# The last tile pair of an fp32-exact MLP: a PSUM bank of its own for one quarter of the result, and bias and residual rows added one chunk pair earlier

## The chip, the cores and the metric

One core of a Trainium2 chip runs the whole program. The metric is device time in microseconds (us), the median of several executions; a single profiled execution supplies the rows that are read here. In the rows, PE is the matrix engine, PEld its weight loads, DVE the vector engine, ACT the scalar engine, POOL the engine that issues one DMA queue, SP the engine that issues another.

## The reference

A transformer block on 2048 tokens of width 640: layer norm with a modulation from `c`, linear attention of 32 heads, a gated residual, then a second layer norm and the MLP. Only the MLP's end is touched:

```
h = jnp.einsum("bsd,df->bsf", x, w1) + b1        # F = 1728
r = jnp.where(h > 0, h, 0);  h = r * r
out = jnp.einsum("bsf,fd->bsd", h, w2) + b2
x = x + gb * out                                  # gb: one row of 640, from c and w_mod
```

## The kernel before

**Tiling.** The MLP works on pairs `j` of token tiles, 8 pairs (`NB`) of 2 x 128 tokens. For each pair the 1728 hidden features are taken in 14 chunks `f` of 128 (the last of 64), two at a time: chunk pair `n` is chunks `2n` and `2n+1`, seven chunk pairs (`NP`) for each `j`. `up(j, f)` makes one chunk of hidden features on PE (15 matmuls of 256 columns; 10 for the last chunk), adds the bias and applies relu on ACT (L1250), squares on DVE (L1251). `split_a` splits the result into a high part (ACT, L1274 and following) and a low part (DVE, L88) because every fp32 product is made of three matmuls, high x high, high x low and low x high (`three`). The tiles that hold these parts are called `ra`, and `ft` before the split. The second product, with `w2`, runs one chunk pair behind and adds into PSUM accumulators.

**Accumulators.** The output of a pair is cut into four quarters, named by letters: `"2"` (tile 0, the 384 left columns), `"3"` (tile 0, the 256 right columns), `"4"` (tile 1, left), `"x"` (tile 1, right). Most chunk pairs use a scheme with seven products instead of eight (`down_pair`), with three further accumulators `"1"`, `"5"`, and `"6"`/`"7"`, whose sums `first_combos` later adds onto the quarters in SBUF, rows `y_0` and `y_1`. For the last pair, `j` = 7, the last three chunk pairs (`n` = 4, 5, 6; `LAST` = 3) use the plain eight products (`down_plain`, and `last_downs` for `n` = 5 and 6). `acc(j, reg)` gives the accumulator of a name. Names of 384 columns have a bank (512 fp32 columns) each; `"3"` and `"x"` share one bank, tile `acc3x` (pool tag `p3x`), and `"6"` and `"7"` share one (tag `p67`). The framework places a wait between an engine that writes a tile and another that reads it; `"3"` and `"x"` are one tile.

**The end of the program.** The engine order is written by hand (`manual_schedule`), in the order of the calls in the loop over `j` and `n`. For `j` = 7 the steps that matter are these, in the words of the kernel:

- `residual(j)` at `n` = 3 puts two DMAs into SP's queue (L1405) that load the residual rows `xr_7_0` and `xr_7_1` (128 x 640 each).
- `add_bias(j, i)` at `n` = 5 adds the prepared row `bb` (gate times b2) to each on DVE.
- `first_combos(j)` at the end of `n` = 4 makes `y_0`, `y_1` from `"1"`, `"5"`, `"6"`, `"7"` (ACT L1424, L1425, then four DVE adds).
- at `n` = 5, `by_gate` (L1418) multiplies both `y` rows by the gate row `gb_b`.
- at `n` = 6, after both `up` and the splits, `add(Y, Y, XR)` (L1415) adds the residual rows to both `y` rows.
- `last_downs` then runs PE through `n` = 5 for `"3"`, `"x"`, `"2"`; `n` = 6 for `"3"`, `"x"`, `"2"`; and `n` = 5 and 6 for `"4"`. As each quarter is complete, DVE multiplies it by the gate into tile `end` (L1418, reading PSUM) and adds it to `y` (L1415), and SP stores it (L1412):

```
        for r in regs:
            if r[0] == "4":
                part(NP - 2, *r)
                at = 0
            part(NP - 1, *r)
            m = r[2].stop - r[2].start
            out_(*r, u[:, at : at + m])
            at += m
```

One line number can belong to many calls: L1415 is every `add`, L1418 every `by_gate`, L78 every matmul, L88 every low part.

Of the kernel before, what the change touches and what calls it, by code (L numbers as in the profile page):

```python
# [8 lines left out]
F32 = mybir.dt.float32  # L9
# [6 lines left out]
P = 128  # L16
# [21 lines left out]
PLAIN = 2  # L38
# [13 lines left out]
def kernel(  # L52
# [23 lines left out]
    def mm(o, terms, first=True, last=True, skip=False):  # L76
        for i, (a, b) in enumerate(terms):
            nc.tensor.matmul(  # L78
                o, a, b,
                start=first and i == 0, stop=last and i == len(terms) - 1,  # L80
                skip_group_check=skip,
            )

    def three(ah, al, bh, bl):
        return [(ah, bh), (ah, bl), (al, bh)]
# [52 lines left out]
    def tp(name):  # L138
        return psA.tile([P, 512], F32, tag="tp", name=name)
# [574 lines left out]
    for t in range(2, NT - 2):  # L714
        j, i = divmod(t, 2)
# [379 lines left out]
    NB = NT // 2  # L1095
# [126 lines left out]
    psC = ctx.enter_context(tc.tile_pool(name="psC", bufs=1, space=PS, reuse_waits="tile"))  # L1222
# [9 lines left out]
    def up(j, f):  # L1232

        n, k = FS[f], f % 2
        alone = j < PLAIN or (j, f) == (NB - 1, NF - 1)
        p = UP2[:, :256] if k and j < PLAIN else tp("up13")[:, :256] if k and alone else UP[:, 256 * k : 256 * k + 256]
        terms = []
        for d in range(NC):
            if n == P:
                terms += three(W1[f][:, 0, d], W1[f][:, 1, d], H2[j][:, d, 0], H2[j][:, d, 1])  # L1240
            else:
                terms += [(W1[f][:, 0, d], H2[j][:, d, 0]), (W1[f][:, 0, d], H2[j][:, d, 1])]
        mm(p, terms, first=(k == 0 or alone), skip=True)
        if k == 0:
            FT[j, f // 2] = p3.tile([P, 8, P], F32, tag="ft", name=f"ft{j}_{f // 2}", bufs=2)
        t = FT[j, f // 2]
        r = t[:, A12 : A22 + 1] if k else t[:, 0:8:7]
        p = p.rearrange("p (i n) -> p i n", i=2)
        if n == P:
            nc.scalar.activation(r, p, AF.Relu, bias=b1_t[:, f : f + 1])  # L1250
            nc.vector.tensor_tensor(r, r, r, op=ALU.mult)  # L1251
        else:
            u = t[:n, S1 : S2 + 1]
            nc.scalar.activation(u, p[n:], AF.Identity, bias=b1_t[n:, f : f + 1])
            nc.vector.tensor_tensor(u, p[:n], u, op=ALU.add)
            nc.vector.scalar_tensor_tensor(r[:n], u, 0.0, u, op0=ALU.max, op1=ALU.mult)

    def plain(j, n):
        return j < PLAIN or n == NF // 2 - 1 or j == NB - 1 and n >= NF // 2 - LAST
# [27 lines left out]
    def split_s(j, n):  # L1287
        t = FT[j, n]
        a = RS[j, n] = p3.tile([P, 2, 4, P], F32, tag="rs", name=f"rs{j}_{n}").bitcast(F32R)
        nc.scalar.activation(a[:, 0], t[:, S1 : S4 + 1], AF.Copy)  # L1290
        lo(a[:, 1], t[:, S1 : S4 + 1], a[:, 0])
# [18 lines left out]
    def t_load(n):  # L1310
        TR_[n] = [row("s1", f"traw{n}_{r}") for r in range(2)]
        for r in range(2):
            f = 2 * n + r
            nc.sync.dma_start(TR_[n][r], w2[f * P : (f + 1) * P])
# [48 lines left out]
    ACC, XR, Y, FIRST = {}, {}, {}, set()  # L1363

    def acc(j, reg):

        bank_ = {"3": "3x", "x": "3x", "6": "67", "7": "67"}.get(reg, reg)
        if (j, bank_) not in ACC:
            if len(bank_) == 2:
                ACC[j, bank_] = psC.tile([P, 512], F32, tag=f"p{bank_}", name=f"acc{bank_}_{j}")  # L1370
            else:
                ACC[j, bank_] = psA.tile([P, 512], F32, tag="pj", name=f"acc{bank_}_{j}", bufs=4)
        t = ACC[j, bank_]
        return (j, bank_), t[:, :384] if len(bank_) == 1 else t[:, 256:] if reg in "x7" else t[:, :256]
# [32 lines left out]
    def add_bias(j, i):  # L1407
        add(XR[j, i], XR[j, i], bb)
# [5 lines left out]
    def add(o, a, b):  # L1414
        nc.vector.tensor_tensor(o, a, b, op=ALU.add)  # L1415

    def by_gate(o, a, c):
        nc.vector.tensor_tensor(o, a, gb_b[:, c], op=ALU.mult)  # L1418
# [56 lines left out]
    def prep(n):  # L1475
        p_hi(n)
        p_lo(n)
        p_load(n)
# [52 lines left out]
    for j in range(NB):  # L1531
        if j <= PLAIN:
            if j:
                by_hand.__exit__(None, None, None)
            by_hand = tc.manual_schedule(engines={ET_.PE, ET_.DVE, ET_.Activation, ET_.Pool} | ({ET_.SP} if j != 1 else set()))
            by_hand.__enter__()
        for n in range(NP):
            down = lambda k: prev and (down_plain if plain(*prev) else down_pair)(*prev, k)
            twice = not plain(j, n)
            m = NP * j + n - NP - 1  # L1540
            if (j, n) == (NB - 1, NP - 1):
                for k in range(2):
                    up(j, 2 * n + k)
                    split_a(j, n, (k,))
                for i in range(2):
                    add(Y[j][i], Y[j][i], XR[j, i])
                break
            done = j - 1 if j and prev else None
            up(j, 2 * n)
            if prev and not plain(*prev):  # L1550
                split_s(*prev)
            down(0)
            if j < PLAIN:
                layer(j + 1, 2 * n, None if j else 0)
            if 0 < m < NP - 2:
                t_split(m - 1)
            if m == -1:
                t_load(0)
            if (j, n) == (PLAIN, 0):
                t_fetch(4)  # L1560
            if j >= PLAIN:
                if n == 5 + (j == PLAIN):
                    for i in range(2):
                        add_bias(j, i)
                layer(j + 1, 2 * n)
            prep(next(PREPS, 0))
            if j == 0:
                layer(j + 1, 2 * n, 1)
            if n == 0 and j:
                if j - 1 >= PLAIN:  # L1570
                    first_combos(j - 1)
                else:
                    Y[j - 1] = [row("s2", f"y{j - 1}_{i}") for i in range(2)]
                for r, i, c in (("3", 0, R), ("2", 0, L)):
                    end(j - 1, r, i, c)
            if n == 1 and j:
                gate(j - 1, 0)
                if j != PLAIN:
                    finish(j - 1, j < PLAIN)
            if n == 1 and j == PLAIN:  # L1580
                finish(j - 1, 0)
            if n == 2 and j == PLAIN:
                t_sums(NP - 2)
            if n == (2 if j > PLAIN else 1) and j:
                gate(j - 1, 1)
            if n == (5, 5, 5, 3)[min(j, 3)]:
                residual(j)
            for i in range(2):
                if n == 6 and j == 0:
                    add_bias(j, i)  # L1590
            if j == NB - 1 and n == 1:
                for k in range(NP - LAST, NP - 1):
                    plain_load(k)
            if j == NB - 1 and n == 3:
                for k in range(NP - LAST, NP - 1):
                    plain_split(k)
            if j == NB - 1 and n == NP - 2:
                for i in range(2):
                    by_gate(Y[j][i], Y[j][i], slice(0, D))
            up(j, 2 * n + 1)  # L1600
            if j >= PLAIN and n == 0:
                down(1)
            split_a(j, n)
            if twice:
                sums(j, n)
            if j < PLAIN or n:
                down(1)
            if m == NP + 1:
                t_split(NP - 2)
            ahead = (j, n) == (0, 3)  # L1610
            if ahead:
                layer(j + 1, 2 * n + 1)
            prep(next(PREPS, 0))
            if n == 0 and j:
                end(j - 1, "4", 1, L)
                end(j - 1, "x", 1, R)
            if n == (2 if j > PLAIN else 1 if j == PLAIN else 0) and j:
                finish(j - 1, j >= PLAIN)
            if not ahead:
                layer(j + 1, 2 * n + 1)  # L1620
            if 0 <= m < NP - 2:
                t_sums(m)
            if m == NP - 2:
                t_split(m - 1)
            if 0 < m + 1 < NP - 1:
                t_load(m + 1)
            if m == NP - 1:
                for i in range(2):
                    add_bias(j - 1, i)
            if j == NB - 1 and n == NP - LAST:  # L1630
                first_combos(j)
            prev = j, n
# [60 lines left out]
```

## Time and profile before

| what | before |
|---|---|
| median of 3 runs (lowest to highest) | 769.94 us (769.52 to 769.98) |
| the profiled execution, its own time | 769.86 us |
| its span in the profile | 768.2 us |
| PE busy | 759.3 us, 99% of the span |
| DVE busy | 593.8 us, 77% |
| ACT busy | 434.6 us, 57% |
| share of the chain that ended last: PE, DVE | 85%, 8% |

The profiled execution's span is 1.7 us shorter than its time; what lies around the span is taken to be the same for both kernels. A timeline row gives start and length of a merged group in us, engine, line, operation, what it writes and reads, its shape and count, and in brackets the idle time of the engine before it and what ended that. PE rows overlap because matmuls are pipelined: the length of a group is from the first start to the last end.

### The profile page before, as it was taken

The page shows a single profiled execution, that of the slowest core. Times are in us where ns is not written, and L with a number is a line of the kernel's source. Part 1 is how long each engine was busy: PE and PEld are TensorE (multiplying, and loading weights), DVE is VectorE, ACT ScalarE, POOL GpSimd, SP SyncE. Part 2 cuts the span into 40 slices and gives each one's busy share as a digit, 9 for nine tenths or more (in the row PEclk, how much of TensorE's full clock was granted, in tenths as well). Part 3 has the DMA queues.
Part 4 walks back from the last instruction along what each step waited for, and adds up shares of the span by engine and source line. Part 5 has one row for each costly group of instructions (what it writes and reads, how often), then busy time and mean ns, then how long its engine had stood idle before and what let it go on. Part 6 is the DMA issues. An engine that isn't in the chain of part 4 may idle for free.

```text
span 768.2 us, 15300 instructions
## 1 busy us (share of the span) xinstructions
PE 759.3 (99%) x5967; PEld 739.8 (96%) x5967; DVE 593.8 (77%) x1083; ACT 434.6 (57%) x971; POOL 144.2 (19%) x301
## 2 busy tenths in 40 slices
PE   9999999999999999999999999999999999999997
PEld 8999999999999989888999999999999999999996
DVE  6598897989999999999565667866767666675666
ACT  5766756767843454545776647465553636445331
POOL 3001101101100255442101000231321313222110
PEclk9999999999999999999999999999999999999999
DMA  9811431343333344155356367996766758766450
GB/s 327 305 65 73 137 103 54 104 139 114 119 104 109 117 142 170 70 80 160 107 180 222 110 226 253 286 323 195 226 181 197 232 177 262 221 184 192 130 165 35
DMA packets 52151, 126.69 MB, mean 165 GB/s; under 512 B 7335, under 2 KB 8103, under 8 KB 52079
## 3 DMA queue, kind: packets, MB, share of 16 engines
q1 hardware_dynamic: 34744, 84.65, 33.1%
q0 software_dynamic: 14752, 35.76, 16.7%
q10 hardware_dynamic: 2583, 5.30, 1.8%
q8 instruction: 47, 0.77, 0.4%
q14 instruction: 25, 0.20, 0.1%
HBM read 95.70 MB, written 29.89 MB: 163 GB/s over the span
## 4 chain that ended last, share of the span: by engine, by line
PE 85%; DVE 8%; issue 2%; DMA 2%; POOL 2%; ACT 1%; SPq 0%; POOLq 0%; DVEq 0%
PE up L78 23%; PE acc L78 17%; PE pk L78 9%; PE pv L78 9%; PE pq L78 8%; PE pwo L78 5%; PE acc3x L78 5%; PE kvp L450 3%; DVE dn L879 2%; DVE scr L877 2%; DVE ezb L901 1%; PE tb L357 1%; PE te L921 1%; DMA ring_b<-td_b 1%; PE ta L357 1%
## 5 line engine op out<-in xcount | busy, mean ns | idle before, releaser
L78 PE MATMUL up<-h,w 128*128 128x256 f32 x1640 | 206.4, 278 | 0.0
L78 PEld LDWEIGHTS up<-h,w 128*128 128x128 f32 x1640 | 196.1, 188 | 0.0
L1250 ACT ACTIVATE ft<-up,b_t 128x256 f32<-128x256 f32 x104 | 48.9, 470 | 115.1 <-PE up L78 114.6
L78 PE MATMUL acc<-w,ra 128*128 128x384 f32 x452 | 97.4, 335 | 0.0
L1251 DVE TENSOR_TENSOR ft<-ft 128x256 f32<-128x256 f32 x104 | 44.1, 424 | 51.2 <-ACT ft L1250 49.6
L78 PE MATMUL pwo<-wo,ot 128*128 128x256 f32 (+3 forms) x512 | 80.8, 312 | 0.6 <-DVE ot L88 0.6
L78 PEld LDWEIGHTS pwo<-wo,ot 128*128 128x128 f32 (+1 forms) x512 | 74.5, 188 | 3.8 <-issue 2.7
L78 PE MATMUL pq<-wq,hT 128*128 128x384 f32 (+1 forms) x480 | 75.2, 312 | 0.0
L78 PEld LDWEIGHTS acc<-w,ra 128*128 128x128 f32 x452 | 72.7, 188 | 0.7 <-DVE ra L88 0.5
L78 PE MATMUL pk<-wk,hT 128*128 128x384 f32 (+1 forms) x480 | 72.7, 308 | 0.0
L78 PE MATMUL pv<-wv,hT 128*128 128x384 f32 (+1 forms) x480 | 71.7, 307 | 0.0
L78 PEld LDWEIGHTS pq<-wq,hT 128*128 128x128 f32 x480 | 71.1, 188 | 0.6 <-issue 0.2
L78 PEld LDWEIGHTS pk<-wk,hT 128*128 128x128 f32 x480 | 70.5, 188 | 0.4 <-issue 0.2
L78 PEld LDWEIGHTS pv<-wv,hT 128*128 128x128 f32 x480 | 70.1, 188 | 0.0
L88 DVE TENSOR_TENSOR ra<-ft,ra 128x384 fp32r<-128x384 f32 (+2 forms) x86 | 36.8, 448 | 32.9 <-ACT ra L1274 20.2
L78 PE MATMUL acc3x<-w,ra 128*128 128x256 f32 x248 | 42.3, 278 | 1.4 <-DVE end L1418 1.4
L1360 POOL DMA_DIRECT2D ring_a<-td_a x34 | 18.3, 537 | 125.5 <-PE acc L78 103.2
L1274 ACT ACTIVATE ra<-ft 128x384 fp32r<-128x384 f32 x48 | 25.2, 526 | 28.4 <-DVE ft L1251 22.4
L78 PEld LDWEIGHTS acc3x<-w,ra 128*128 128x128 f32 x248 | 39.5, 188 | 1.8 <-DVE end L1418 1.6
L1265 DVE TENSOR_TENSOR ft<-ft 128x128 f32<-128x128 f32 x136 | 33.3, 286 | 1.2
L441 DVE TENSOR_REDUCE sk<-ek 128x64 f32<-128x1280 f32 x16 | 23.7, 1484 | 12.4 <-ACT ek L436 10.8
L885 POOL TENSOR_TENSOR dn<-dn,rs_q 128x32 f32<-128x32 f32 x32 | 20.1, 629 | 68.1 <-DVE dn L879 67.8
(264 smaller groups left out, 1406.5 us busy)
## 6 DMA issues: line engine op xcount, KB each, us to landing
ring_c<-td_c POOLq DMA_DIRECT2D x34, 384.0 KB, 4.0
ring_a<-td_a POOLq DMA_DIRECT2D x34, 384.0 KB, 4.1
ring_b<-td_b POOLq DMA_DIRECT2D x34, 256.0 KB, 4.0
esp<-eq SPq DMA_DIRECT2D x12, 640.0 KB, 3.2
el<-esp SPq DMA_DIRECT2D x12, 640.0 KB, 4.0
rw<-in_w SPq DMA_DIRECT2D x23, 320.0 KB, 3.1
wm<-in_w_mod SPq DMA_DIRECT2D x20, 320.0 KB, 3.7
xb<-in_x SPq DMA_DIRECT2D x8, 640.0 KB, 4.0
```

What stands on the lines that cost most here:

```text
L78: nc.tensor.matmul(o, a, b, start=first and i == 0, stop=last and i == len(terms) - 1, skip_group_check=skip,)
L88: (eng or nc.vector).tensor_tensor(out_lo, full, hi.bitcast(F32), op=ALU.subtract)
L357: nc.tensor.transpose(p[:, i * P : (i + 1) * P], xn[:, i, d * P : (d + 1) * P], ident)
L441: nc.vector.tensor_reduce(s, heads(flat(e)), axis=AX.X, op=ALU.add)
L450: nc.tensor.matmul(kvp[g // 4][64 * c : 64 * c + 64, a : a + 2 * n].rearrange("p (s n) -> p s n", s=2), v[:, u], e[:, :, o : o + n], start ...
L877: nc.vector.tensor_tensor(z, flat(ET[t]), flat(zb), op=ALU.mult)
L885: nc.gpsimd.tensor_tensor(dn[:, s], dn[:, s], rs[:, 1 - s], op=ALU.mult)
L1250: nc.scalar.activation(r, p, AF.Relu, bias=b1_t[:, f : f + 1])
L1251: nc.vector.tensor_tensor(r, r, r, op=ALU.mult)
L1265: nc.vector.tensor_tensor(t[:, o], t[:, a], t[:, b], op=op)
L1274: nc.scalar.activation(a[:, 0, :3], t[:, :3], AF.Copy)
L1360: nc.gpsimd.dma_start(RING[j, n, r], TD[n][r].bitcast(F32R))
```

## The change

`acc` gives quarter `"x"` of the last pair a tile of its own, `accx`, in the bank of the tag `p67`, which `"6"` and `"7"` of that pair have left after `first_combos`. `add_bias` of the last pair goes from `n` = 5 to `n` = 4 (there it stands behind the low part of `split_s` and ahead of `up(7, 9)`'s square). The addition of the residual rows goes from `n` = 6 to `n` = 5, each right behind its `by_gate`. No instruction is added or removed; pairs 0 to 6 are untouched.

```diff
     def acc(j, reg):
 
+        if (j, reg) == (NB - 1, "x"):
+            if (j, reg) not in ACC:
+                ACC[j, reg] = psC.tile([P, 512], F32, tag="p67", name="accx")
+            return (j, reg), ACC[j, reg][:, :256]
         bank_ = {"3": "3x", "x": "3x", "6": "67", "7": "67"}.get(reg, reg)
@@
                     up(j, 2 * n + k)
                     split_a(j, n, (k,))
-                for i in range(2):
-                    add(Y[j][i], Y[j][i], XR[j, i])
                 break
@@
             if j >= PLAIN:
-                if n == 5 + (j == PLAIN):
+                if n == 5 + (j == PLAIN) - (j == NB - 1):
                     for i in range(2):
                         add_bias(j, i)
@@
             if j == NB - 1 and n == NP - 2:
                 for i in range(2):
                     by_gate(Y[j][i], Y[j][i], slice(0, D))
+                    add(Y[j][i], Y[j][i], XR[j, i])
```

On PE the place is the end of the program, from the first products of `ra_6` (`n` = 6) on: `"3"`, then `"x"`. Before, with the semaphores that each row waits for:

```order
L78 MATMUL acc3x_9076<-w_12_5160,ra_6_9396 128x256 [waits Activation_49]
L78 MATMUL acc3x_9076<-w_12_5160,ra_6_9396 128x256
L78 MATMUL acc3x_9076<-w_12_5160,ra_6_9396 128x256 [waits DVE_49]
L78 MATMUL acc3x_9076<-w_13_5163,ra_6_9396 128x256 [waits DVE_49]
L78 MATMUL acc3x_9076<-w_13_5163,ra_6_9396 128x256
L78 MATMUL acc3x_9076<-w_12_5160,ra_6_9396 128x256 [waits DVE_49]
L78 MATMUL acc3x_9076<-w_12_5160,ra_6_9396 128x256 x2
L78 MATMUL acc3x_9076<-w_13_5163,ra_6_9396 128x256 x2
```

The sixth row is the first product of `"x"` in this chunk pair; it waits on DVE for the read of `"3"` out of the same tile. The same place in the changed kernel:

```order
L78 MATMUL acc3x_9076<-w_12_5160,ra_6_9399 128x256 [waits Activation_49]
L78 MATMUL acc3x_9076<-w_12_5160,ra_6_9399 128x256
L78 MATMUL acc3x_9076<-w_12_5160,ra_6_9399 128x256 [waits DVE_49]
L78 MATMUL acc3x_9076<-w_13_5163,ra_6_9399 128x256 [waits DVE_49]
L78 MATMUL acc3x_9076<-w_13_5163,ra_6_9399 128x256
L78 MATMUL accx<-w_12_5160,ra_6_9399 128x256 x3
L78 MATMUL accx<-w_13_5163,ra_6_9399 128x256 x2
```

The order of the products is the same; those of `"x"` write `accx` and carry no wait. The first product of `"x"` altogether stands in chunk pair 5 (it is the second product of `n` = 4), where it now waits on DVE for `first_combos`.

On DVE the first place is chunk pair 4, around the squares of `up(7, 8)` and `up(7, 9)` (both `ft_4`) with the low part of `split_s` (`rs_3`) between them. Before:

```order
L1251 TENSOR_TENSOR ft_4_9253<-ft_4_9253 128x2x128
L88 TENSOR_TENSOR rs_3_9256<-ft_3_9175,rs_3_9256 128x512
L1251 TENSOR_TENSOR ft_4_9253<-ft_4_9253 128x256
L88 TENSOR_TENSOR ra_4_9285<-ft_4_9253,ra_4_9285 128x384
L88 TENSOR_TENSOR ra_4_9285<-ft_4_9253,ra_4_9285 128x128
```

In the changed kernel:

```order
L1251 TENSOR_TENSOR ft_4_9253<-ft_4_9253 128x2x128
L88 TENSOR_TENSOR rs_3_9256<-ft_3_9175,rs_3_9256 128x512
L1419 TENSOR_TENSOR xr_7_0_9192<-xr_7_0_9192,bb 128x640
L1419 TENSOR_TENSOR xr_7_1_9194<-xr_7_1_9194,bb 128x640
L1251 TENSOR_TENSOR ft_4_9253<-ft_4_9253 128x256
L88 TENSOR_TENSOR ra_4_9287<-ft_4_9253,ra_4_9287 128x384
L88 TENSOR_TENSOR ra_4_9287<-ft_4_9253,ra_4_9287 128x128
```

The two bias additions, each behind its own DMA, now stand ahead of the second square (`add` is L1419 there). The second place on DVE is chunk pair 5, between its two squares (`ft_5`). Before:

```order
L1251 TENSOR_TENSOR ft_5_9325<-ft_5_9325 128x2x128
L1415 TENSOR_TENSOR xr_7_0_9192<-xr_7_0_9192,bb 128x640
L1415 TENSOR_TENSOR xr_7_1_9194<-xr_7_1_9194,bb 128x640
L1418 TENSOR_TENSOR y_0_9302<-y_0_9302,gb_b 128x640
L1418 TENSOR_TENSOR y_1_9303<-y_1_9303,gb_b 128x640
L1251 TENSOR_TENSOR ft_5_9325<-ft_5_9325 128x256
```

In the changed kernel:

```order
L1251 TENSOR_TENSOR ft_5_9327<-ft_5_9327 128x2x128
L1422 TENSOR_TENSOR y_0_9304<-y_0_9304,gb_b 128x640
L1419 TENSOR_TENSOR y_0_9304<-y_0_9304,xr_7_0_9192 128x640
L1422 TENSOR_TENSOR y_1_9305<-y_1_9305,gb_b 128x640
L1419 TENSOR_TENSOR y_1_9305<-y_1_9305,xr_7_1_9194 128x640
L1251 TENSOR_TENSOR ft_5_9327<-ft_5_9327 128x256
```

Two rows have left and two have come from the end, so four rows of 640 columns stand here as before, the additions each behind the gate product whose result they read. At the end, the read of `"3"` into `end` follows the last low part (`ra_6`) directly; the two additions that stood between them are gone. ACT, POOL and SP have the same rows in the same order.

## The prediction

> **What bounds the kernel now.** I read the page's busy shares first, then the waits of the last 28 us, then the chain that ended last, then single rows of the end. The shares:
>
> ```profile
> PE 759.3 (99%) x5967; PEld 739.8 (96%) x5967; DVE 593.8 (77%) x1083; ACT 434.6 (57%) x971; POOL 144.2 (19%) x301
> ```
>
> PE has no spare time to speak of, so an edit gains only where PE stands, or behind PE's last matmul. The waits in the window from 740 us on give, of all engines, for PE only this (engine and line, waited for: total, times, longest):
>
> ```profile
> PE acc3x L78 <- DVE end L1418: 1.4, 1, 1.4
> ```
>
> One stop, of PE behind DVE's gate product. The chain that ended last shows what that stop consists of (start, length):
>
> ```profile
> 758.03 0.42 DVE ra L88
> 758.45 0.03 issue
> 758.48 1.56 DVE y L1415 x2
> 760.04 0.34 DVE end L1418
> 760.38 0.04 issue
> 760.43 0.84 PE acc3x L78 x5
> 761.26 2.79 PE acc L78 x16
> 764.05 0.02 issue
> 764.07 0.57 DVE end L1418
> ```
>
> The reader is to see that the chain leaves PE for two DVE steps, the two residual additions (758.48) and the read of "3" (760.04), and comes back to the five products of "x". The timeline rows of the same place:
>
> ```profile
> 758.00 1.00 PE L78 MATMUL acc3x<-w,ra 128*128 128x256 f32 x5
> 758.50 0.30 PEld L78 LDWEIGHTS acc3x<-w,ra 128*128 128x128 f32 x2 [0.20 <-DVE ra L88]
> 759.96 0.42 DVE L1418 TENSOR_TENSOR end<-acc3x,gb_b 128x256 f32<-128x256 f32 x1
> 760.41 0.42 DVE L1415 TENSOR_TENSOR y<-y,end 128x256 f32<-128x256 f32 x1
> 760.43 0.84 PE L78 MATMUL acc3x<-w,ra 128*128 128x256 f32 x5 [1.43 <-DVE end L1418]
> 761.30 0.43 DVE L1418 TENSOR_TENSOR end<-acc3x,gb_b 128x256 f32<-128x256 f32 x1 [0.47 <-PE acc3x L78]
> 761.76 0.42 DVE L1415 TENSOR_TENSOR y<-y,end 128x256 f32<-128x256 f32 x1
> 762.16 0.56 DVE L1418 TENSOR_TENSOR end<-acc,gb_b 128x384 f32<-128x384 f32 x1
> 762.76 0.56 DVE L1415 TENSOR_TENSOR y<-y,end 128x384 f32<-128x384 f32 x1
> ```
>
> PE ends "3" at 759.00, stands 1.43 us, and runs "x" from 760.43 to 761.27.
>
> **The change, part by part. The bank.** "x" no longer waits for the read of "3". The idle 1.43 us goes. That isn't all: a group that starts from a standstill is slower than one that follows others. A flowing group and the first matmul after the stop:
>
> ```profile
> 755.60 1.52 PE L78 MATMUL acc3x<-w,ra 128*128 128x256 f32 x12
> 760.43 0.38 PE L78 MATMUL acc3x<-w,ra 128*128 128x256 f32 x1 [1.43 <-DVE end L1418]
> L78 PE MATMUL acc3x<-w,ra 128*128 128x256 f32 x248 | 42.3, 278 | 1.4 <-DVE end L1418 1.4
> ```
>
> The twelve take 1.52 us, and one matmul of this shape lasts 278 ns on average (the third row, of the page's costliest groups), so the ends are (1.52 - 0.28) / 11 = 0.113 us apart. In flow the five of "x" would end 5 x 0.113 = 0.57 us behind those of "3", at 759.57; now they end at 761.27. The gain on PE is **1.70 us**: 1.43 of idle time and 0.27 of restart (0.84 - 0.57, the first matmul alone 0.38). The bounds: 1.43, if the restart is only a matter of how ends are modelled and comes back elsewhere, and 1.70. I take 1.70, since the chain's own row for "x" has 0.84, and the last low part (758.45) is already in when the five would start.
>
> On the restart a rule of the Trainium skill gives another figure. "TensorE: Matmul & The Clock Gate", in its sections on single matmul latency and on the back-to-back issue gap, puts a lone warm matmul of N columns at (398 + N) / 2.4 ns and the following ones N / 2.4 + 2.5 ns apart: an estimate of 272 and 109 ns for N = 256. By it the restart costs 0.16 us and the sum would be 1.59 us. The spacing agrees with the trace's 113 ns; the first matmul after the stop does not, 0.38 us here, and the trace decides.
>
> The other 16 products follow in 2.79 us as now: 759.57 + 2.79 = 762.36 instead of 764.05. Nothing new holds them: the operands of "2" and "4" were made before.
>
> **The wait that is added.** The first product into accx waits for first_combos, since the bank was that of "6" and "7". Rows of chunk pair 5:
>
> ```profile
> 746.79 1.83 DVE L1415 TENSOR_TENSOR y<-y,acc 128x256 f32<-128x256 f32 x4
> 747.63 0.68 PE L78 MATMUL acc<-w,ra 128*128 128x384 f32 x3
> 751.56 0.51 PE L78 MATMUL acc3x<-w,ra 128*128 128x256 f32 x3
> ```
>
> first_combos ends at 748.62, the first product of "x" runs at 751.56: 2.9 us of cover. If it were gone, everything on PE would queue behind it.
>
> **The bias rows, one chunk pair earlier.** Two DVE additions of 640 columns, whose place in chunk pair 4 is a hole:
>
> ```profile
> 742.41 0.69 DVE L88 TENSOR_TENSOR rs<-ft,rs 128x512 fp32r<-128x512 f32 x1
> 745.09 0.43 DVE L1251 TENSOR_TENSOR ft<-ft 128x256 f32<-128x256 f32 x1 [1.99 <-ACT ft L1250]
> 746.11 0.76 DVE L88 TENSOR_TENSOR ra<-ft,ra 128x384 fp32r<-128x384 f32 x2 [0.59 <-PE acc L78]
> 748.88 1.55 DVE L1415 TENSOR_TENSOR xr<-xr,bb 128x640 f32<-128x640 f32 x2
> 750.35 1.55 DVE L1418 TENSOR_TENSOR y<-y,gb_b 128x640 f32<-128x640 f32 x2
> 751.82 0.42 DVE L1251 TENSOR_TENSOR ft<-ft 128x256 f32<-128x256 f32 x1
> ```
>
> They take 1.55 us and DVE stands idle for 1.99 us from 743.10. They cost nothing if the residual rows have landed by 745.09 - 1.55 = 743.54. Behind that lies more cover: the low parts of pair 4 end at 746.87 and PE's first product with them starts at 747.63, 0.76 us later, so the limit is a landing at 744.30. SP's issues, the landing times of such transfers on the page, and the DMA traffic:
>
> ```profile
> 735.79 1.10 SPq L1405 DMA_DIRECT2D xr<-x  x2
> xr<-x SPq DMA_DIRECT2D x16, 320.0 KB, 4.6
> rawv<-in_wv SPq DMA_DIRECT2D x5, 320.0 KB, 10.6
> 742.00:743.00 1.00, 1.00 (x8) 1.00 (x8) 0.91 (x2) 0.38 (x1) 0.00 (x0) 1.00 0.20 47
> 743.00:744.00 1.00, 1.00 (x11) 1.00 (x10) 0.11 (x1) 0.00 (x0) 0.00 (x0) 1.00 0.02 6
> 744.00:745.00 1.00, 1.00 (x9) 1.00 (x9) 0.00 (x0) 0.41 (x1) 0.00 (x0) 1.00 0.00 0
> ```
>
> The second issue starts at about 736.34; with the median of 4.6 us it lands at 740.9. The last number of a window row is GB/s: from 744.00 on nothing is moving, so no landing is later than that. Cost 0 at both bounds, because even 744.00 is ahead of 744.30.
>
> **The residual additions, from the end into chunk pair 5.** There the bias rows have left, so four rows of 640 columns stand there as before, from 748.88 to the square at 751.82. Two of them now follow the row that they read. Rows that depend on each other start 0.04 us after the end (762.16 + 0.56, then 762.76), independent ones start 0.73 us apart (1.55 - 0.82). So 2 x 0.86 + 2 x 0.73 = 3.18 us against 2.94: the square comes 0.24 us later and ends at 752.48. Who waits for it is ACT:
>
> ```profile
> 752.97 0.53 ACT L1274 ACTIVATE ra<-ft 128x384 fp32r<-128x384 f32 x1 [1.25 <-PE acc3x L78]
> ```
>
> ACT waits for PE to leave the old ra until 752.97, so 0.49 us of cover hide it. At the end, 1.56 us of DVE in front of the read of "3" go: it starts at 759.03 instead of 759.96. With the distances of the rows above (0.45, 0.40, 0.46, 0.40, 0.60, and 0.56 for the last) DVE's six steps for "3", "x", "2" start at 759.03, 759.48, 759.88, 760.34, 760.74 and 761.34 and end at 761.90. "4" is complete at 762.36: DVE is ready 0.46 us ahead, PE sets the end, and all of the 1.70 arrives. The last addition ends at 763.52 instead of 765.22; the last store behind it stays as it is.
>
> **Sum** against the profiled execution: 769.86 - 1.70 = 768.16 us. That execution is 0.08 us under the median of the runs shown; against the median it is 768.24. I forecast **768.2**, 0.22% less.
>
> **Rivals.** *The restart is no gain:* only the idle time of 1.43 goes, 769.86 - 1.43 = 768.4. For it: ends of matmuls are modelled; against: DVE's read of "x" starts at 761.30, an event of another engine that confirms the end at 761.27. Chance 0.14.
>
> *The wait stays in another form* (the change does not do what it says: "x" still starts behind the read of "3"). Then only the additions help: the read ends at 759.45, "x" starts at 759.50 instead of 760.43, gain 0.93, 768.9. Against: the rows of the changed order carry no such wait. Chance 0.06. Its mirror image, where the additions still stand in front of the read of "3" in time, would let PE finish "4" at 762.36 but DVE come to "4" only at 759.96 + 0.45 + 0.40 + 0.46 + 0.40 + 0.60 + 0.60 = 762.87 instead of 764.07: gain 1.20, 768.7. Chance 0.04.
>
> *Slower: the residual rows are late.* DVE works in order, so an addition that waits for its DMA holds the square, the split and then PE. Each us of landing behind 744.30 is a us of PE. The gain is used up at 746.00. If they took what the slowest weight loads took, 10.6 us, they would land at 746.9: 2.6 us of stall, 0.9 net, 770.8. Against: the windows above show the transfers over by 744.00. Chance 0.04.
>
> **How the numbers follow.** My forecast has the other 0.72. A measurement of this kernel can tell about 0.2% from no change, 1.54 us, which is a time under 768.4, and the forecast lies only 0.16 us beyond. Within my own case I give four chances in five of landing under it, since the three runs shown lie within 0.46 us (0.58); the first rival lies just on the other side of the line (0.02 of its 0.14), the next two are inside it, and the slow rival is mostly inside it as well (0.11% at its price; half of its chance goes beyond). Faster by over 0.2%: 0.60; within: 0.38; slower: 0.02. The range is from 767.9, the forecast with the scatter of runs, to 768.9, which takes in both bounds of the restart and the rival in which the wait stays.
>
> **What would show each step.** The changed profile should have no PE wait on DVE end; the group of "x" should merge with that of "3" on PE without idle time; the residual additions should stand in front of the square of chunk pair 5, ending by 752.5, and the bias additions in the hole before 745.1, with no DMA wait named; the read of "3" should start within 0.1 us of 759.0, and DVE should wait for PE before the last gate product by about 0.5 us; the last addition should end about 1.70 us ahead of its old place. Wrong would be: an idle time of DVE in front of the bias rows, a PE wait around 747.6 or 751.6, a DVE row for "4" that starts later than 762.4, or a last store that takes longer to land.

## The result, and the profile after

| | before | after |
|---|---|---|
| median of 11 runs each (lowest to highest) | 769.98 us (769.07 to 771.25) | 767.88 us (767.04 to 768.97) |
| the profiled execution, its span | 769.86 us, 768.2 us | 767.73 us, 766.0 us |

The ratio is 0.9976, 95% interval 0.9968 to 0.9984: the change makes the kernel faster by 0.24%, 2.1 us between the medians (the interval is 1.2 to 2.5 us). The forecast was 768.2 us. Two executions of those below, one of "x" last and one of the kernel before, took twice as long (1537 and 1538 us; in the one with a trace, 25 matmuls of `up` take 6.05 us against 3.00) and enter no comparison.

The waits of the last 26 us of the changed kernel no longer contain a wait of the matmuls for DVE; instead the gate products on DVE (L1422 in this kernel, the additions are L1419) wait for PE, twice 0.6 us:

```profile
DVE end L1422 <- PE acc L78: 0.6, 1, 0.6
DVE end L1422 <- PE acc3x L78: 0.6, 1, 0.6
```

The chain that ended last now stays on PE until "4" is complete:

```profile
757.71 0.34 PE acc3x L78 x3
758.06 0.00 issue
758.06 0.51 PE acc3x L78 x2
758.57 0.57 PE accx L78 x5
759.14 2.79 PE acc L78 x16
761.92 0.02 issue
761.95 0.57 DVE end L1422
762.51 0.02 issue
762.54 0.56 DVE y L1419
```

The five products of "x" took 0.84 us behind an idle 1.43; they now take 0.57 directly behind "3". The two DVE steps that stood in the chain are gone from it. DVE's timeline of the end:

```profile
757.58 0.42 DVE L88 TENSOR_TENSOR ra<-ft,ra 64x256 fp32r<-64x256 f32 x1 [0.48 <-ACT ra L1284]
758.60 0.42 DVE L1422 TENSOR_TENSOR end<-acc3x,gb_b 128x256 f32<-128x256 f32 x1 [0.60 <-PE acc3x L78]
759.06 0.43 DVE L1419 TENSOR_TENSOR y<-y,end 128x256 f32<-128x256 f32 x1
759.40 0.42 DVE L1422 TENSOR_TENSOR end<-accx,gb_b 128x256 f32<-128x256 f32 x1
761.95 0.56 DVE L1422 TENSOR_TENSOR end<-acc,gb_b 128x384 f32<-128x384 f32 x1 [0.60 <-PE acc L78]
762.54 0.56 DVE L1419 TENSOR_TENSOR y<-y,end 128x384 f32<-128x384 f32 x1
```

A measure inside the trace, which leaves out all that happens earlier, is the **stretch** from the start of the last low part to the end of the last addition: 758.03 to 765.22 before, 7.19 us; 757.58 to 763.10 after, 5.52 us. The end gained **1.67 us**. The other part of the lead of this pair of traces, 0.45 us (758.03 against 757.58), is already there at the last low part; most of it is one wait of PE, at 515 us of the program, in before and in after:

```profile
PE acc L78 <- DMA ring_b<-td_b: 0.7, 1, 0.7
```

```profile
PE acc L78 <- DMA ring_b<-td_b: 0.3, 1, 0.3
```

That is a wait for a weight transfer in an earlier pair, which the change does not touch. In the traces of the runs below it is between 0 and 1.1 us.

The moved rows stand where the order put them:

```profile
742.58 1.55 DVE L1419 TENSOR_TENSOR xr<-xr,bb 128x640 f32<-128x640 f32 x2
744.65 0.43 DVE L1251 TENSOR_TENSOR ft<-ft 128x256 f32<-128x256 f32 x1 [0.52 <-ACT ft L1250]
748.44 0.82 DVE L1422 TENSOR_TENSOR y<-y,gb_b 128x640 f32<-128x640 f32 x1
749.29 0.82 DVE L1419 TENSOR_TENSOR y<-y,xr 128x640 f32<-128x640 f32 x1
750.03 0.82 DVE L1422 TENSOR_TENSOR y<-y,gb_b 128x640 f32<-128x640 f32 x1
750.88 0.82 DVE L1419 TENSOR_TENSOR y<-y,xr 128x640 f32<-128x640 f32 x1
751.63 0.42 DVE L1251 TENSOR_TENSOR ft<-ft 128x256 f32<-128x256 f32 x1
```

The bias rows fill the hole of chunk pair 4 (0.52 of its 1.99 us is left) without an idle time in front of them, and the four rows of chunk pair 5 take 3.19 us up to the square.

### The profile page after: what moved, and what is told of

Its sections match the earlier page's. It is cut to its first block, busy times and chain, and to the rows that moved or that the text cites. A ratio compares the mean times of both kernels' runs of the same rounds, so it can differ in the third digit from the quotient of the medians.

```text
span 766.0 us, 15300 instructions
## 1 busy us (share of the span) xinstructions
PE 759.3 (99%) x5967; PEld 740.1 (97%) x5967; DVE 594.1 (78%) x1083; ACT 434.9 (57%) x971; POOL 144.4 (19%) x301
## 4 chain that ended last, share of the span: by engine, by line
PE 87%; DVE 5%; DMA 3%; issue 2%; ACT 1%; POOL 0%; SPq 0%; POOLq 0%; DVEq 0%; ACTq 0%
PE up L78 21%; PE acc L78 16%; PE pq L78 9%; PE pk L78 9%; PE pv L78 9%; PE pwo L78 7%; PE acc3x L78 4%; PE kvp L450 3%; PE te L921 2%; PE tb L357 1%; DMA raw_q<-in_wq 1%; DMA ring_b<-td_b 1%; PE ta L357 1%; PE numa L78 1%; PE foldq L280 1%
## 5 line engine op out<-in xcount | busy, mean ns | idle before, releaser
L1274 ACT ACTIVATE ra<-ft 128x384 fp32r<-128x384 f32 x48 | 25.2, 526 | 28.4 <-DVE ft L1251 22.4
L78 PE MATMUL acc3x<-w,ra 128*128 128x256 f32 x231 | 39.8, 278 | 0.0
L78 PEld LDWEIGHTS acc3x<-w,ra 128*128 128x128 f32 x231 | 37.2, 188 | 0.2 <-DVE ra L88 0.2
```

The source lines that it names most:

```text
L78: nc.tensor.matmul(o, a, b, start=first and i == 0, stop=last and i == len(terms) - 1, skip_group_check=skip,)
L1274: nc.scalar.activation(a[:, 0, :3], t[:, :3], AF.Copy)
```

## The experiments

Each run's time is given with its ratio to the kernel before on the same chip. Since a median of some ten runs is known here to about 0.1%, the stretch in the trace tells more than the times.

### The bank alone

Against the kernel before, only `acc` is changed:

```diff
     def acc(j, reg):
 
+        if (j, reg) == (NB - 1, "x"):
+            if (j, reg) not in ACC:
+                ACC[j, reg] = psC.tile([P, 512], F32, tag="p67", name="accx")
+            return (j, reg), ACC[j, reg][:, :256]
```

Expected:

> The bank for "x" alone; bias and residual additions stay where they were. Measured inside the trace from the start of the last low part on DVE to the end of the last addition: 7.19 us before, 5.52 after the whole change. My theory (two parts that need each other): PE does not wait any more and finishes "4" as early as with the whole change, but DVE reads "3" only behind the two residual additions, about 1.5 us behind the low part, and then is itself the bound for "4": stretch 5.7 to 6.0 us, gain 1.2 to 1.5 us. Rival (the wait was all): 5.5 us, gain 1.7. Rival (the additions were all): 7.2 us, no gain.

Measured: 768.07 us, ratio 0.9978 (0.9969 to 0.9987), stretch 757.72 to 763.44, **5.72 us**, as expected. Rows of DVE's end in this kernel (the addition behind the read of "3" and the two rows of "x" are left out), and PE's last group:

```profile
758.17 1.56 DVE L1419 TENSOR_TENSOR y<-y,xr 128x640 f32<-128x640 f32 x2
759.65 0.42 DVE L1422 TENSOR_TENSOR end<-acc3x,gb_b 128x256 f32<-128x256 f32 x1
761.24 0.55 DVE L1422 TENSOR_TENSOR end<-acc,gb_b 128x384 f32<-128x384 f32 x1
761.82 0.56 DVE L1419 TENSOR_TENSOR y<-y,end 128x384 f32<-128x384 f32 x1
762.30 0.55 DVE L1422 TENSOR_TENSOR end<-acc,gb_b 128x384 f32<-128x384 f32 x1
762.88 0.56 DVE L1419 TENSOR_TENSOR y<-y,end 128x384 f32<-128x384 f32 x1
```

```profile
759.11 2.93 PE L78 MATMUL acc<-w,ra 128*128 128x384 f32 x16
```

No row has an idle time in brackets: DVE is busy without a gap from the low part to the end and has become the bound, while PE finished "4" at 759.11 + 2.93 = 762.04, 0.26 us before DVE came to it. The bank by itself is worth 1.47 us, and 0.20 us are left to the rows.

### The moved rows alone

The whole change without the four lines above. Expected:

> The bias and residual additions moved as in the change, "3" and "x" still in one bank. My theory: the wait stays, but ends with a read of "3" that starts 0.9 us sooner; PE's idle time is 0.5 us instead of 1.43 and the restart of 0.27 us is still paid: stretch 6.2 to 6.3 us, gain about 0.9 us. Rival (the wait was all): 7.2 us, no gain. Rival (the additions were all): 5.5 us, gain 1.7.

Measured: 768.44 us, ratio 0.9988 (0.9979 to 0.9997), stretch 758.10 to 764.43, **6.33 us**, just over the expected 6.2 to 6.3. PE's rows:

```profile
758.07 1.01 PE L78 MATMUL acc3x<-w,ra 128*128 128x256 f32 x5
759.59 0.85 PE L78 MATMUL acc3x<-w,ra 128*128 128x256 f32 x5 [0.52 <-DVE end L1418]
```

The wait stays, 0.52 us long, and so does the slow start behind it (0.85 us for five). The rows are worth 0.86 us by themselves. So the parts alone give 1.47 and 0.86, together 1.67. The bank removes PE's wait and the rows shorten it, which is why the sum is too much; the rows also take work from DVE, the bound once the wait is gone, which is why the bank alone is not enough.

### Another order in place of the bank

The moved rows without the bank; in `last_downs`, second loop:

```diff
-        for r in regs:
+        for r in (regs[0], regs[2], regs[1], regs[3]):
```

Expected:

> The additions moved as in the change, "3" and "x" still in one bank, but in the last chunk pair PE runs "3", "2", "x", "4" in place of "3", "x", "2", "4". If the bank matters only through the wait, the five products of "2" (0.87 us) cover the read of "3" (0.46 us behind its end) and nothing else changes: no PE wait, stretch 5.5 us, gain 1.7 us as with the bank. If a bank of its own is worth something by itself (reads of one half slow the writes into the other), the products of "x" or the gate products are longer here and the stretch lies above 5.6.

Measured: 767.88 us, ratio 0.9982 (0.9973 to 0.9991), stretch 758.54 to 764.07, **5.53 us**. "3" and "x" share a bank here, with "2" between them:

```profile
758.51 1.01 PE L78 MATMUL acc3x<-w,ra 128*128 128x256 f32 x5
759.36 1.03 PE L78 MATMUL acc<-w,ra 128*128 128x384 f32 x5
760.23 0.75 PE L78 MATMUL acc3x<-w,ra 128*128 128x256 f32 x5
760.82 2.07 PE L78 MATMUL acc<-w,ra 128*128 128x384 f32 x11
```

There is no idle time on PE, and the stretch equals the changed kernel's to 0.01 us. The bank is worth the wait and the restart that it removes and shows no gain besides; products that are put between the two users of one bank do the same.

### "x" last

The whole change, with the last quarter made the narrow one (the lines that are left out write the last addition out in place, which gives it the line L1465, and change nothing else):

```diff
-        regs = ("3", 0, R), ("x", 1, R), ("2", 0, L), ("4", 1, L)
+        regs = ("3", 0, R), ("2", 0, L), ("4", 1, L), ("x", 1, R)
         for r in regs[:3]:
             part(NP - 2, *r)
         for r in regs:
-            if r[0] == "4":
+            if r[0] == "x":
```

Expected:

> The whole change, and PE's order at the end is "3", "2", "4" for chunk pair 5, then "3", "2", "4" for chunk pair 6, then both chunk pairs of "x": the last quarter has 256 columns in place of 384. PE's work is the same. Theory: behind PE's last product DVE has 0.42 + 0.42 us in place of 0.56 + 0.56, and DVE comes free for the last gate product at about the time that PE ends: stretch 5.0 to 5.2 us, 0.3 to 0.5 less than with the change. Rival: DVE becomes the bound, since "4" is read shortly ahead of "x" (1.2 us for gate and addition): stretch 5.5 us or more, no gain over the change.

The trace is that of the execution of 1537 us, so there is no stretch from this run. Its other five times have a median of 767.17 us and give a ratio of 0.9971 (0.9959 to 0.9984). The same kernel again:

> The same kernel as in the run with "x" last, for a trace at full matmul speed. Theory: stretch from the start of the last low part to the end of the last addition 5.0 to 5.2 us, 0.3 to 0.5 less than with the change (5.52). Rival (DVE is the bound behind "4"): 5.5 us or more.

Measured: 767.44 us, ratio 0.9969 (0.9957 to 0.9981), stretch 756.61 to 761.58, **4.97 us**:

```profile
759.25 1.41 PE L78 MATMUL accx<-w,ra 128*128 128x256 f32 x11
```

```profile
757.72 0.42 DVE L1422 TENSOR_TENSOR end<-acc3x,gb_b 128x256 f32<-128x256 f32 x1 [0.69 <-PE acc3x L78]
759.65 0.55 DVE L1422 TENSOR_TENSOR end<-acc,gb_b 128x384 f32<-128x384 f32 x1
760.23 0.56 DVE L1465 TENSOR_TENSOR y<-y,end 128x384 f32<-128x384 f32 x1
760.71 0.42 DVE L1422 TENSOR_TENSOR end<-accx,gb_b 128x256 f32<-128x256 f32 x1
761.16 0.42 DVE L1465 TENSOR_TENSOR y<-y,end 128x256 f32<-128x256 f32 x1
```

PE ends "x" at 760.66 and DVE reaches it at 760.71, with no idle time since the read of "3": the two come out even, and the narrow quarter saves 0.55 us over the change, slightly more than the 0.3 to 0.5 expected.

### The bias rows alone

Of the change only `n == 5 + (j == PLAIN) - (j == NB - 1)`. Expected:

> Of the change only the bias additions, one chunk pair earlier; bank and residual additions as before. Theory (the hole of 1.99 us in chunk pair 4 hides them, and nothing gains from it at the end): stretch 7.2 us as before, PE idle 1.4 us in front of "x", no DVE idle time in front of the bias rows, time within the scatter of before. Rival (the earlier place costs something): the square behind them starts more than 0.4 us after ACT has its input, and PE waits in chunk pair 5.

Measured: 769.39 us, ratio 0.9997 (0.9988 to 1.0006), stretch 757.30 to 764.52, 7.22 us, PE's idle time 1.43 us. The additions start at 742.29 without an idle time before them. Alone the early place neither costs nor gains anything.

### The bias rows at their load

The slow rival, provoked: the whole change, with both bias additions of the last pair directly behind `residual(j)` in chunk pair 3.

```diff
-                if n == 5 + (j == PLAIN) - (j == NB - 1):
+                if n == 5 + (j == PLAIN) and j < NB - 1:
                     for i in range(2):
                         add_bias(j, i)
@@
             if n == (5, 5, 5, 3)[min(j, 3)]:
                 residual(j)
+                if j == NB - 1:
+                    for i in range(2):
+                        add_bias(j, i)
```

Expected:

> The whole change, but the bias additions stand directly behind the issue of their loads, in chunk pair 3, about one and a half chunk pairs earlier still. This tries the slow rival of the prediction (DVE held by a late DMA holds PE). Theory: DVE stands idle until the rows land, 4 to 5 us behind the issue (median of such loads 4.6 us), the square of the second chunk of pair 3 comes about 3.5 to 4 us late, and PE, which has 1 to 1.5 us of cover there, stops for 2 to 3 us: 770 to 771 us. It also dates the landing, which the prediction put at 740.9 us. Rival (loads land in time, or the cover is larger): less than 1 us of PE wait, 768 us.

Measured: one time of 772.12 us. DVE's and PE's waits, from 730 us on:

```profile
DVE xr L1419 <- DMA xr<-x: 3.5, 2, 3.2
PE acc L78 <- ACT ra L1274: 2.1, 1, 2.1
```

PE's stop is as expected, the loss is not: from the square of chunk 6 of this pair to the last low part the kernel takes 761.93 - 735.09 = 26.84 us against 757.58 - 734.95 = 22.63 with the change, 4.2 us more. The rest stands in the column of the granted clock (the number behind PE's count; then DMA share and GB/s):

```profile
742.00:743.00 1.00, 0.00 (x0) 1.00 0.03 8
743.00:744.00 1.00, 0.92 (x4) 1.00 0.00 0
744.00:745.00 1.00, 1.00 (x5) 0.55 0.00 0
745.00:746.00 1.00, 1.00 (x5) 0.50 0.00 0
746.00:747.00 1.00, 1.00 (x6) 0.50 0.00 0
747.00:748.00 1.00, 1.00 (x9) 0.75 0.00 0
748.00:749.00 1.00, 1.00 (x9) 1.00 0.00 0
```

One us behind the restart at 743.08 the clock falls to 0.50 for (0.45 + 0.50 + 0.50 + 0.25) / 0.50 = 3.4 us, which costs half of that, 1.7 us, on top of 2.1 us of stop and about 0.25 of restart (the 0.27 measured at the end of the kernel before, taken as an estimate here): 4.05 of the 4.2. The same kernel again:

> The same kernel as in the run with the bias additions at the load, timed in rounds and traced again. There PE stopped for 2.10 us and then ran at a granted clock of 0.50 for 3.4 us. If the half clock is what a stop of this length brings, every execution has it: about 4.4 us over the change, 771.5 to 773 us. If it depends on where the stop falls, the times fall into two groups, about 2.4 us and about 4.2 us over the change, 770 and 772.

Measured: 772.93 us (772.41 to 774.79, 4 runs), ratio 1.0049 (1.0034 to 1.0064). The first row landed later in this trace (740.88 against 739.47), PE stopped 3.52 us, and the clock fell again, here 0.1 us behind the restart at 744.23:

```profile
744.00:745.00 1.00, 0.77 (x3) 0.67 0.00 0
```

The same sum, 3.52 + 1.7 + 0.25 = 5.47, meets a loss of 5.45 us between the same two rows (762.90 - 734.82 = 28.08, less 22.63). No execution was near 770. That does not show that every one ran at the half clock: 3.4 us of it make a mean granted clock of 0.998, which three of the five executions with both rows at the load have, but one of 774.79 us has 0.994 and one of 772.41 us has 1.000 (the kernel before lists 0.999 or 1.000 throughout).

### One bias row at its load

Only the first of the two additions stands behind the load, the second in chunk pair 4:

> The whole change, but the first of the two bias additions stands directly behind the issue of its load in chunk pair 3, the second in chunk pair 4. DVE is held until the first row lands, about 1.2 us less than with both. Theory: PE stops 0.8 to 1.1 us, the clock stays at 1.00, and the loss against the change is the stop and a restart of about 0.25 us: stop plus 0.1 to 0.4 us, 768.7 to 769.4 us. Rival: any stop lowers the clock, and the loss is 2.5 us or more.

Measured: 771.47 us (770.07 to 772.51, 8 runs), ratio 1.0025 (1.0013 to 1.0037). The expectation failed: the first row landed at 740.94 in this trace against 739.47 in the first of these three, PE stopped 2.40 us and not 1, and the clock fell to 0.50 again, 0.1 us behind the restart at 743.38:

```profile
743.00:744.00 1.00, 0.62 (x2) 0.76 0.07 8
```

The sum is 2.40 + 1.7 + 0.25 = 4.35 us for a loss of 4.28 (762.00 - 735.09 = 26.91, less 22.63). The eight times fall in two: 770.07 to 770.84 us in three executions with a mean granted clock of 0.999 or 1.000, 771.23 to 772.51 us in five with 0.996 to 0.998. So the three seem to have kept the full clock; they have no trace, and how long PE stopped in them is not known. A stop of about 1 us at this place was therefore not tried. Shorter stops with a trace are the 1.43 us of before and of the bias rows alone, the 0.52 us of the rows alone, and, earlier in the program, 1.10 us behind ring_b in the run with another order; while PE worked on behind them the clock stayed at 1.00.

### One residual addition left at the end

> The whole change, but one of the two residual additions (0.82 us) stays at the end, in front of the read of "3". Theory: DVE idles 0.60 us there and again 0.60 us in front of the last gate product with the change, so the read of "3" starts 0.15 to 0.2 us later and "4" not at all: stretch 5.5 us, PE sets the end. Rival (every DVE us at the end counts): stretch 5.7 to 6.2 us.

Here one of the two residual additions stays in front of the read of "3". Measured: one time of 766.6 us, stretch 756.43 to 761.95, **5.52 us**, the changed kernel's to the hundredth:

```profile
756.88 0.82 DVE L1419 TENSOR_TENSOR y<-y,xr 128x640 f32<-128x640 f32 x1
757.63 0.42 DVE L1422 TENSOR_TENSOR end<-acc3x,gb_b 128x256 f32<-128x256 f32 x1
760.79 0.56 DVE L1422 TENSOR_TENSOR end<-acc,gb_b 128x384 f32<-128x384 f32 x1 [0.44 <-PE acc L78]
```

The read of "3" comes 0.18 us later than with the change (1.20 us behind the start of the last low part against 1.02), the idle time in front of "4" shrinks from 0.60 to 0.44, and the end does not move.

### The change again, beside "x" last

> The changed kernel as it is, in the same call as the others. Theory: stretch from the start of the last low part to the end of the last addition 5.5 us again, 1.67 under before, and the rest of its lead in time (2.1 us between the medians) is scatter from DMA waits: PE waits for ring_b between 0 and 1.1 us in the traces so far. Its lead is then nearer to 1.7 than to 2.1. Rival: the change gains something ahead of the end too; then the lead stays over 2.0 and the trace shows a PE wait ahead of 740 us that before has in every execution and this kernel in none.

> The kernel with "x" last, beside the changed kernel on the same chip. Theory: stretch 4.97 us as in its last trace, 0.55 under the change; time 0.3 to 0.8 us under the changed kernel's median. Rival: no difference in time, since something behind the last addition (the store) makes up for it.

Measured: the change 767.50 us, ratio 0.9978 (0.9970 to 0.9987), stretch 757.04 to 762.56, 5.52 us; its lead is 1.71 us here, with a ring_b wait of 0.2 us in its trace. "x" last 766.68 us, ratio 0.9963 (0.9950 to 0.9976), stretch 757.26 to 762.24, 4.98 us. In its three runs the ratio of "x" last was 0.9971, 0.9969 and 0.9963, that of the change 0.9976 and 0.9978; each pair of intervals overlaps. Side by side as here, four of the five times of "x" last lie below all twelve of the change, and the medians are 0.82 us apart where 0.3 to 0.8 was expected. The traces give 0.54 us for the end; the rest is within the scatter.

## Why the prediction was right, point by point

- **The restart belongs to the gain.** Right: 0.84 us became 0.57, and the stretch shrank by 1.67 where 1.43 of idle time went (forecast 1.70). The rival in which the restart is no gain, 1.43, is 0.24 off in a measure whose repeats agree to 0.03 (5.52 and 5.52, 4.97 and 4.98; 7.19 and, with the bias rows alone, 7.22). The estimate from the Trainium skill's figures ("TensorE: Matmul & The Clock Gate", sections on single matmul latency and on the back-to-back issue gap) was 1.59; 1.67 lies nearer to the 1.70 that the trace's own rows gave.
- **The added wait has cover.** Right: no PE wait in chunk pair 5; with the bank alone there is none either.
- **The bias rows cost nothing.** Right, alone and together. Their cover was smaller than the prediction's landing at 740.9 made it: with the additions at the load the second row landed at 740.64 in one trace and at about 741.8 in another, and the changed kernel's first addition starts at 742.58, 0.8 us behind that.
- **The residual rows fit into chunk pair 5.** Right: 3.19 us for a forecast of 3.18, hidden, as ACT's L1274 still waits for PE.
- **PE sets the end, DVE is ready ahead of it.** Right, by 0.60 us where 0.46 was forecast: steps that wait for nothing start 0.34 us apart (759.06 to 759.40), and the prediction had used 0.40, a distance that held a wait (by the spacing of PE's products "2" was complete at about 762.13 there, and DVE's row starts at 762.16). The same mistake made the rival in which the additions still stand in front of the read too dear: 1.20 us of gain for PE without the wait and DVE as the bound, 1.47 measured with the bank alone, where those two steps are 0.34 and the last one 0.48 instead of 0.60.
- **The slow rival** did not happen, but its price was wrong: "Each us of landing behind 744.30 is a us of PE" leaves out the restart and the clock. A stop of 2.1 us cost 4.2.
- **The last store.** The prediction named a later landing as a sign of being wrong; the span ends 768.2 - 765.22 = 2.98 us behind the last addition before and 766.0 - 763.10 = 2.90 after.
- **The total.** 768.2 forecast, 767.88 measured, at the lower edge of the range that began at 767.9. The gain of the first runs, 2.1 us, holds about 0.4 us that the mechanism does not explain: the second set of runs gave a lead of 1.71 us, and PE's wait for ring_b moves by up to 1.1 us from one trace to the next. That part of the gain is scatter, not foresight.

## What to carry to other kernels

Where two results share a PSUM bank, look at what PE does between the last product of the one and the first of the other: a bank of its own and other products in between gave the same 1.67 us, both with the reader freed of the two additions. With them still in front of it the bank gave 1.47; the other order was not tried so. A PE wait costs its length and a restart (here 0.27 us for a group of five), so the idle column understates it. Of two edits that attack one wait, cost each alone and both together; here they gave 1.47, 0.86 and 1.67.

## What the runs showed of the hardware

A stop of PE can cost twice its length: stops of 2.10, 2.40 and 3.52 us cost 4.2, 4.3 and 5.45 us. Stops of 0.52, 1.10 and 1.43 us left the granted clock at 1.00; those of 2.10, 2.40 and 3.52 us were each followed by about 3.4 us at 0.50. The Trainium skill ("TensorE: Matmul & The Clock Gate", Part 1) says that the clock falls after an idle window of about 3.4 us. The length of the slow time agrees with that window; the length of the stop does not, since 2.10 us were enough here.

A limit between 1.43 and 2.10 us can't be read off these stops, because the same idle time does not always end in the same way. The fall came 1.0 us behind the restart in one trace and 0.1 us in two, which is 3.1, 3.6 and 2.5 us behind the start of the stop. At the end of the program, where PE has nothing left, the clock fell 2.2 us behind the last product in the run with one residual addition left (at 762.96, last product to 760.76), but was still at 1.00 in the kernel before when its span ended, 4.2 us behind the last product (764.03 to 768.2). So the moment of a stop seems to count besides its length; what sets that moment stays open.
